# Decode block with grouped-query attention: value product 512 columns wide on two groups of 64 output partitions, and 21 instead of 14 rows of w_down summed 512 columns wide

## The chip, the cores and the metric

The kernel runs on one NeuronCore of one Trainium2 chip. The metric is the device time of one launch in microseconds (us), lower is better. The kernel before takes 437.93 us, the median of 3 runs (437.82 to 437.97).

## What is computed

One decode step of a transformer block for 8 batch rows of width 1024. A modulation product turns `c` into six shift, scale and gate rows; then come attention with a key/value cache, and a gated feed-forward part:

```python
mod = silu(c) @ w_mod                        # 1024 x 6144: sa, ca, ga, sb, cb, gb
h = layernorm(x) * (1 + ca) + sa
q = h @ wq                                   # 32 heads of 128
scores = einsum('bhqd,bhkd->bhqk', q, k) * 128 ** -0.5   # 4 kv heads, 8192 positions, 8 query heads each
o = einsum('bhqk,bhkd->bhqd', softmax(scores), v)
x = x + ga * (o @ wo)
h = layernorm(x) * (1 + cb) + sb
gate = h @ W_gate; up = h @ W_up             # 1024 x 3584
x = x + gb * ((gate * (gate > 0) * up) @ W_down)         # 3584 x 1024
```

All inputs are bf16. The key and value caches hold 67 MB each, the weights 51.4 MB together, so 185.6 MB are read once.

## The kernel before

**Loading.** SyncE's queue issues every large load, in one fixed order (L347-382, issued at L745), into a ring of five SBUF slots A to E of 32 KB per partition: both halves of wq, both of w_mod, then keys of pair 0, and then for each pair n the keys of n+1 and the values of n; wo's first half stands behind the values of pair 0. After the values of pair 15 come wo's second half, the first halves of W_gate and W_up, the second halves, and w_down in five blocks of 14, 7, 4, 2 and 1 rows (a "row" here is one of 28 chunks of 128 contraction rows, `WD`, L380). A load waits until TensorE's last use of what lay in its place before: the keys of pair n+2 until the keys of pair n have been transposed, the values of n+2 until the value product of n is done, wo's second half until the keys of pair 14 are done, the first half of W_gate until the keys of pair 15 are. The queue is served in order, so what stands behind a waiting load waits too.

**Attention.** A pair is one batch row and two of the four key/value heads: 16 pairs, each with 4.19 MB of keys and as much of values. The loop (L646-682) has 18 turns; 16 of them run as a hardware loop of 8 rounds with two turns each, and two more follow without keys. Turn n works on three pairs at once. It transposes the keys of pair n on TensorE, 128 transposes in 16 slots of 8 (`slot_keys`), which VectorE and ScalarE copy out alternately; after every second slot it forms scores (`slot_scores`: 4 products of 512 columns, each writing 32 output partitions of one PSUM bank). It runs the softmax of pair n-1 in slots 2 to 8 (`soft_max` to `turn_p`), and the value product of pair n-1 from slot 9 on (`pv`, eight calls, the last two in slot 15). And it finishes pair n-2: `pv_evac` in slot 0 (two VectorE operations from PSUM bank W into `od`), `o_sum` in slot 2 (TensorE, which needs `od`), `o_evac` in slot 3. The order on every engine is the order in which the code records the operations. The calls in odd slots 9, 11, 13 and 15 stand right behind four score products.

**Value product.** The probabilities are transposed into `pt`, 16 blocks t of 128 positions' columns. For each t four products run, one per group of 32 output partitions, each with 32 columns of `pt` as weights and 256 columns of values (L616-619). Of each result only one 128-column half belongs to the right positions; `pv_evac` masks with `diag` and sums the two halves (L621-623).

**Feed-forward tail.** Gate and up are multiplied with h as they land (L698-703), the product of relu(gate) and up is transposed into `hmT`. w_down's first 14 rows are summed 512 columns wide in four groups of 32 output partitions (bank Y, L722-726); that sum is copied to `yR` by VectorE, and two TensorE products with `fold` bring it into bank W (L727-729). The other 14 rows, in blocks of 7, 4, 2 and 1, are added in W as four products of 256 columns each (L730-734). Two VectorE operations and four small DMAs write the output (L735-739).

Of the kernel before, what the change touches and what calls it, by code (L numbers as in the profile page):

```python
# [234 lines left out]
def bass_adaLN_cond__gqa_block_cached__glu_gated_reglu__decode_kernel(  # L235
# [33 lines left out]
    with ExitStack() as es:  # L269
        E = es.enter_context  # L270

        def sb(name, shape, dtype):
            return E(nc.sbuf_tensor(name, shape, dtype))
# [24 lines left out]
        nb = sb("nb", [128, 1], f32)  # L298
        P = sb("P", [128, 1088], bf16)
        pt = sb("pt", [128, 2048], bf16)  # L300
        ov = sb("ov", [128, 256], f32)
        od = sb("od", [128, 132], f32)
        rl = sb("rl", [128, 1], f32)
        tm = sb("tm", [128, 128], f32)
        sel = sb("sel", [128, 128], f32)
        selo = sb("selo", [128, 128], f32)
        sel16 = sb("sel16", [128, 16], f32)
        diag = sb("diag", [128, 2, 128], bf16)
        blk = sb("blk", [128, 8, 16], f32)
        pick = sb("pick", [128, 2, B], f32)  # L310
        fold = sb("fold", [128, 2, 128], f32)
# [115 lines left out]
        def dve(name, *args, reads=(), writes=(), **kw):  # L427
            return g.op("dve", lambda e: getattr(e, name)(*args, **kw), reads, writes)  # L428
# [19 lines left out]
        def spread(view, n, tile, key, axes=AX.X):  # L448
            dve("tensor_reduce", sel16[:, 0:n], view, axes, ALU.add, reads=["identf"], writes=["sel16"])
            dve("tensor_copy", tile[:].rearrange("p (a z) -> p a z", a=n) if len(tile.shape) == 2 else tile[:],  # L450
                sel16[:, 0:n, None].to_broadcast([128, n, tile.shape[-1] if len(tile.shape) == 3 else tile.shape[-1] // n]),
                reads=["sel16"], writes=[key])

        spread(identf[:].rearrange("p (g y h) -> p g h y", g=2, y=8), 16, sel, "sel")
        spread(identf[:].rearrange("p (q g i h) -> p g h q i", q=4, g=2, i=2), 16, selo, "selo", AX.XY)
        spread(identf[:].rearrange("p (q i r) -> p i q r", q=8, i=2), 2, diag, "diag", AX.XY)
        spread(identf[:].rearrange("p (y k) -> p k y", k=8), 8, blk, "blk")
        dve("tensor_reduce", part[:], identf[:].rearrange("p (q x) -> p q x", q=4), AX.X, ALU.add, reads=["identf"], writes=["part"])
        dve("tensor_reduce", rest[:], identf[:].rearrange("p (q x) -> p x q", q=4), AX.X, ALU.add, reads=["identf"], writes=["rest"])
# [153 lines left out]
        def pv(n, u):  # L613
            v = place[("v", n)].rearrange("p (h j q e) d -> p h q e j d", h=2, j=4, q=2)
            for t in (2 * u, 2 * u + 1):
                for q in range(4):  # L616
                    at = 32 * (4 * t + q)
                    mm(W[32 * q:32 * (q + 1), 0:256], pt[:, at:at + 32], v[:, t // 8, q // 2, t % 8, 2 * (q % 2):2 * (q % 2) + 2, :],
                       t == 0, t == 15, [("pt", t // 8, 0), ("pt", t // 8, 1)], [pW], ("v", n))

        def pv_evac(n):  # L621
            dve("tensor_tensor", out=ov[:, 0:256], in0=W[:, 0:256], in1=diag[:].rearrange("p i d -> p (i d)"), op=ALU.mult, reads=[pW, "diag"], writes=["ov"])
            dve("tensor_reduce", od[:, 0:128], ov[:, 0:256].rearrange("p (i d) -> p d i", i=2), AX.X, ALU.add, reads=["ov"], writes=["od"])

        def o_sum(n):
            mm(W[:, 0:128], selo[:], od[:, 0:128], True, True, ["selo", "od"], [pW])
# [92 lines left out]
        def hm(r):  # L719
            return hmT[:, r // 4, r % 4, :]  # L720

        for t in range(14):  # L722
            w = place[("wd", 0)][:, t, :]
            for h in range(2):
                at = 64 * (t % 2) + 32 * h
                mm(Y[at:at + B, :], hm(t), w[:, 512 * h:512 * (h + 1)], t < 2, t >= 12, [("hmT", 0)], [pY], ("wd", 0))
        dve("tensor_copy", yR[:], Y, reads=[pY], writes=["yR"])  # L727
        for i in range(2):
            mm(W[:, 0:256], fold[:, i], yR[:, 256 * i:256 * (i + 1)], i == 0, False, ["yR", "fold"], [pW])
        for u, (lo, hi, _) in enumerate(WD[1:], 1):  # L730
            for r in range(lo, hi):
                for q in range(4):
                    mm(W[32 * q:32 * q + B, 0:256], hm(r), place[("wd", u)][:, r - lo, 256 * q:256 * (q + 1)], False, r == KF - 1,
                       [("hmT", r // 16)], [pW], ("wd", u))
# [47 lines left out]
```

## Time and profile before

| | |
|---|---|
| median of 3 runs | 437.93 us |
| span of the profiled execution, first to last instruction | 436.1 us |
| TensorE matmul busy | 305.4 us (70%) |
| VectorE busy, ScalarE busy | 180.2 us (41%), 208.6 us (48%) |
| HBM read, mean rate over the span | 185.63 MB, 426 GB/s |
| share of the 16 DMA engines taken by the load queue | 98.8% |

The profiled execution is told by its span; what lies around it is not on the page, and the median of the runs is 1.8 us above the span. Three views carry the rest. The timeline lists instructions in order of time, merged when they are alike (`x8` is eight in a row), with the idle time before them and what ended it. The view of windows gives busy time per engine, granted TensorE clock and DMA rate in stretches of the span. The chain lists what ended last, step by step. In all of them L420 is the helper that records every product, L424 the one for transposes, L428 VectorE's and L431 ScalarE's, so instructions are told apart by their tiles: `ring,pt` is the value product, `KT,Z` the scores, `identb,ring` the key transposes, `ring,hmT` w_down.

### The profile page before, as it was taken

The numbers are of one execution on the slowest core, as the hardware profiler recorded it, in microseconds if no ns is written. First come the engines' busy times: TensorE is split into PE (matmuls) and PEld (weight loads), VectorE is DVE, ScalarE is ACT, GpSimd is POOL, SyncE is SP. The second block draws the span as 40 slices with busy tenths as digits, with TensorE's granted clock in tenths as the row PEclk, the third lists the DMA queues.
The fourth block names the chain that finished last, engine by engine and source line by source line (L and its number), as shares of the span: only waits on it lengthen the run. The fifth ranks groups of instructions, "written<-read, shape, count | busy, mean of one in ns | idle before, by whom it ended". The sixth has DMA issues, their size and how long they took to land.

```text
span 436.1 us, 10694 instructions
## 1 busy us (share of the span) xinstructions
PE 305.4 (70%) x4560; PEld 199.2 (46%) x4560; DVE 180.2 (41%) x385; ACT 208.6 (48%) x246; POOL 12.6 (3%) x52
## 2 busy tenths in 40 slices
PE   0104257989878888787888888777888878754463
PEld 0101025656555555554555555555555555431321
DVE  3600036456363644536264553536364453331111
ACT  2200005576756747675664757576575747400000
POOL 6000000000000000000000000000000000000000
PEclk9999599999999999999999999999999999885778
DMA  8999999999999999999999999999999999999996
GB/s 346 440 437 437 428 431 432 431 434 428 436 433 433 433 433 433 433 436 433 433 433 433 433 433 433 433 433 433 439 436 433 436 433 433 424 428 429 442 416 253
DMA packets 6874, 185.80 MB, mean 426 GB/s; under 512 B 800, under 2 KB 832, under 8 KB 1104
## 3 DMA queue, kind: packets, MB, share of 16 engines
q1 hardware_dynamic: 6800, 185.61, 98.8%
q8 instruction: 8, 0.13, 0.1%
q10 hardware_dynamic: 64, 0.04, 0.0%
q14 instruction: 2, 0.02, 0.0%
HBM read 185.63 MB, written 0.02 MB: 426 GB/s over the span
## 4 chain that ended last, share of the span: by engine, by line
DMA 58%; PE 20%; issue 8%; DVE 7%; ACT 5%; SPq 1%; DVEq 0%; ACTq 0%
DMA ring<-in_A_k_cache_dram 34%; DMA ring<-in_w_mod_dram 11%; PE PS L424 11%; PE PS L420 10%; DMA ring<-in_B_W_up_dram 6%; DMA ring<-in_B_W_down_dram 6%; ACT P L431 3%; DVE KT L428 2%; ACT KT L431 2%; DVE tm L428 1%; DVE ov L428 1%; DVE nm L428 1%; SPq L745 1%; DVE nb L428 0%; DVE rl L428 0%
## 5 line engine op out<-in xcount | busy, mean ns | idle before, releaser
L431 ACT ACTIVATE KT<-PS 128x1024 bf16<-128x1024 bf16 (+1 forms) x130 | 132.1, 1017 | 165.8 <-PE PS L424 137.6
L424 PE MATMUL PS<-identb,ring 128*128 128x128 bf16 x2048 | 152.9, 220 | 21.8 <-DMA ring<-in_A_k_cache_dram 20.1
L428 DVE COPY KT<-PS 128x1024 bf16<-128x1024 bf16 (+1 forms) x129 | 88.9, 689 | 164.3 <-PE PS L424 128.9
L424 PEld LDWEIGHTS PS<-identb,ring 128*128 128x128 bf16 x2048 | 117.0, 98 | 61.0 <-issue 36.9
L420 PE MATMUL PS<-KT,Z 128*32 128x512 bf16 x516 | 51.9, 389 | 0.1
L420 PE MATMUL PS<-ring,pt 128*32 128x256 bf16 x1088 | 49.9, 274 | 0.3 <-DVE pt L428 0.3
L431 ACT ACTIVATE P<-PS,nb 64x1024 bf16<-64x1024 f32 x34 | 37.7, 1108 | 6.2 <-DVE nb L428 4.2
L424 PE MATMUL PS<-identb,P 128*128 128x128 bf16 x272 | 21.6, 225 | 20.2 <-ACT P L431 14.5
L420 PEld LDWEIGHTS PS<-ring,pt 128*32 128x32 bf16 x1088 | 24.4, 95 | 12.7 <-issue 0.5
L420 PE MATMUL PS<-ring,siluT 128*24 128x512 bf16 x96 | 9.1, 555 | 27.4 <-DMA ring<-in_w_mod_dram 27.4
L424 PEld LDWEIGHTS PS<-identb,P 128*128 128x128 bf16 x272 | 16.0, 100 | 26.5 <-DVE KT L428 17.2
L431 ACT ACTIVATE pt<-PS 64x512 bf16<-64x512 bf16 x34 | 20.1, 591 | 13.5 <-PE PS L424 13.3
L428 DVE COPY pt<-PS 64x512 bf16<-64x512 bf16 x34 | 14.4, 422 | 17.4 <-PE PS L424 16.9
L428 DVE TENSOR_REDUCE mp<-PS 128x1 f32<-128x1024 f32 x17 | 20.6, 1214 | 0.0
L420 PE MATMUL PS<-ring,h2T 128*8 128x512 bf16 x112 | 12.0, 545 | 11.9 <-DMA ring<-in_B_W_up_dram 10.1
L420 PEld LDWEIGHTS PS<-KT,Z 128*32 128x32 bf16 x516 | 13.3, 92 | 13.8 <-ACT KT L431 0.5
L420 PEld LDWEIGHTS PS<-ring,siluT 128*24 128x24 bf16 x96 | 3.0, 124 | 33.2 <-DMA ring<-in_w_mod_dram 28.1
L431 ACT ACT_TABLE_LOAD x11 | 14.1, 1283 | 8.5 <-DMA KT<-in_A_x_dram 8.3
L424 PE MATMUL PS<-identb,KT 128*128 128x128 bf16 (+1 forms) x20 | 1.9, 218 | 18.0 <-DVE KT L428 18.0
L635 POOL CAST ot<-og 128x16 bf16<-128x16 f32 x16 | 4.1, 253 | 290.5 <-DVE og L428 290.5
L420 PEld LDWEIGHTS PS<-ring,h2T 128*8 128x8 bf16 x112 | 3.4, 104 | 19.8 <-DMA ring<-in_B_W_up_dram 11.5
L420 PE MATMUL PS<-od,selo 128*128 128x128 f32 x36 | 8.8, 326 | 5.1 <-DVE od L428 5.1
(99 smaller groups left out, 157.5 us busy)
## 6 DMA issues: line engine op xcount, KB each, us to landing
ring<-in_A_k_cache_dram SPq DMA_DIRECT2D x16, 4096.0 KB, 21.6
ring<-in_A_v_cache_dram SPq DMA_DIRECT2D x16, 4096.0 KB, 30.5
ring<-in_w_mod_dram SPq DMA_DIRECT2D x2, 6144.0 KB, 42.5
ring<-in_A_wq_dram SPq DMA_DIRECT2D x2, 4096.0 KB, 16.9
ring<-in_A_wo_dram SPq DMA_DIRECT2D x2, 4096.0 KB, 29.4
ring<-in_B_W_gate_dram SPq DMA_DIRECT2D x2, 3584.0 KB, 25.0
ring<-in_B_W_up_dram SPq DMA_DIRECT2D x2, 3584.0 KB, 31.1
ring<-in_B_W_down_dram SPq DMA_DIRECT2D x1, 3584.0 KB, 37.6
```

Source lines behind the costliest of these rows:

```text
L420: return pe(lambda e: e.matmul(out_, lhsT, rhs, start=start, stop=stop, skip_group_check=True), reads, writes, block, deps)
L424: return pe(lambda e: e.matmul(out_, in_, ident, start=True, stop=True, is_transpose=True), reads, writes, block)
L428: return g.op("dve", lambda e: getattr(e, name)(*args, **kw), reads, writes)
L431: return g.op("act", lambda e: e.activation(*args, **kw), reads, writes)
L635: pool(lambda e: e.tensor_copy(dst, og[:, n % 2]), reads=[("og", n % 2)], writes=[("ot", n // B)])
L745: o.fn = (lambda e, key=key, src=src, o=o: e.dma_start(place[key], src).then_inc(o.sem, 16))
```

## The change

For each block t the value product is two products instead of four: 64 columns of `pt` as weights, 64 output partitions, 512 columns of values. The bank W then holds four 128-column parts per partition of which one belongs to it. So `ov` and `diag` are twice as wide, `pv_evac` masks 512 columns and sums four parts, and the mask is built by two reductions and two multiplications at the start instead of one reduction and one copy. In the tail, w_down's rows 0 to 20 (its first two blocks) are summed 512 columns wide in bank Y, and the copy to `yR` and the two `fold` products follow row 20 instead of row 13; rows 21 to 27 stay as they were. TensorE's program, loop counted once, is 2,015 instructions long, by 220 shorter than before.

```diff
-        ov = sb("ov", [128, 256], f32)
+        ov = sb("ov", [128, 512], f32)
-        diag = sb("diag", [128, 2, 128], bf16)
+        diag = sb("diag", [128, 2, 2, 128], bf16)
+        pair = sb("pair", [128, 2, 2], f32)
...
-        spread(identf[:].rearrange("p (q i r) -> p i q r", q=8, i=2), 2, diag, "diag", AX.XY)
+        dve("tensor_reduce", pair[:, 0], identf[:].rearrange("p (q a r) -> p a q r", q=2, a=2), AX.XY, ALU.add, reads=["identf"], writes=["pair0"])
+        dve("tensor_reduce", pair[:, 1], identf[:].rearrange("p (q i r) -> p i q r", q=8, i=2), AX.XY, ALU.add, reads=["identf"], writes=["pair1"])
+        for a in range(2):
+            dve("tensor_scalar", out=diag[:, a], in0=pair[:, 1, :, None].to_broadcast([128, 2, 128]), scalar1=pair[:, 0, a:a + 1], scalar2=None,
+                op0=ALU.mult, reads=["pair0", "pair1"], writes=["diag"])
...
-                for q in range(4):
-                    at = 32 * (4 * t + q)
-                    mm(W[32 * q:32 * (q + 1), 0:256], pt[:, at:at + 32], v[:, t // 8, q // 2, t % 8, 2 * (q % 2):2 * (q % 2) + 2, :],
+                for q in range(2):
+                    at = 64 * (2 * t + q)
+                    mm(W[64 * q:64 * (q + 1), :], pt[:, at:at + 64], v[:, t // 8, q, t % 8],
                        t == 0, t == 15, [("pt", t // 8, 0), ("pt", t // 8, 1)], [pW], ("v", n))
...
-            dve("tensor_tensor", out=ov[:, 0:256], in0=W[:, 0:256], in1=diag[:].rearrange("p i d -> p (i d)"), op=ALU.mult, reads=[pW, "diag"], writes=["ov"])
-            dve("tensor_reduce", od[:, 0:128], ov[:, 0:256].rearrange("p (i d) -> p d i", i=2), AX.X, ALU.add, reads=["ov"], writes=["od"])
+            dve("tensor_tensor", out=ov[:], in0=W[:], in1=diag[:].rearrange("p a i d -> p (a i d)"), op=ALU.mult, reads=[pW, "diag"], writes=["ov"])
+            dve("tensor_reduce", od[:, 0:128], ov[:].rearrange("p (i d) -> p d i", i=4), AX.X, ALU.add, reads=["ov"], writes=["od"])
...
-        for t in range(14):
-            w = place[("wd", 0)][:, t, :]
+        for t in range(21):
+            u = t // 14
+            w = place[("wd", u)][:, t % 14, :]
             for h in range(2):
                 at = 64 * (t % 2) + 32 * h
-                mm(Y[at:at + B, :], hm(t), w[:, 512 * h:512 * (h + 1)], t < 2, t >= 12, [("hmT", 0)], [pY], ("wd", 0))
+                mm(Y[at:at + B, :], hm(t), w[:, 512 * h:512 * (h + 1)], t < 2, t >= 19, [("hmT", t // 16)], [pY], ("wd", u))
...
-        for u, (lo, hi, _) in enumerate(WD[1:], 1):
+        for u, (lo, hi, _) in enumerate(WD[2:], 2):
```

## The prediction, made before the result was known

> **What bounds the kernel now.** I read the page first (queues, 40 slices), then the waits of SyncE's queue and its timeline, then TensorE's and VectorE's timeline of one turn of the loop.
>
> ```profile
> q1 hardware_dynamic: 6800, 185.61, 98.8%
> HBM read 185.63 MB, written 0.02 MB: 426 GB/s over the span
> 0.00:2.00 2.00, 0.00 (x0) 0.00 (x0) 0.00 (x0) 0.00 (x0) 1.47 (x12) 1.00 0.67 188
> 254.00:292.00 38.00, 30.95 (x488) 21.03 (x481) 18.49 (x38) 24.76 (x29) 0.67 (x4) 1.00 1.01 438
> ```
>
> The load queue fills 98.8% of the span. So the time changes only if the last load lands at another time, or if the work behind it does. The queue starves only if TensorE frees a slot too late. SyncE's timeline tells how late it is now:
>
> ```profile
> 83.17 0.33 SPq L745 DMA_DIRECT2D ring<-in_A_k_cache_dram  x1
> 100.90 0.33 SPq L745 DMA_DIRECT2D ring<-in_A_k_cache_dram  x1
> 118.64 0.33 SPq L745 DMA_DIRECT2D ring<-in_A_k_cache_dram  x1
> 332.15 19.62 SPq L745 DMA_DIRECT2D ring<-in_A_v_cache_dram  x2
> 370.10 0.33 SPq L745 DMA_DIRECT2D ring<-in_B_W_gate_dram  x1
> ```
>
> The first three rows are the moments at which the keys of pairs 0, 1 and 2 are used up: 17.73 and 17.74 us apart. There TensorE runs behind the loads and at its own pace, so one turn of its own takes 17.73 us. Later one turn takes 19.36 us ((370.10 - 118.64) / 13 = 19.34 to the keys of pair 15), which is 8.39 MB at 433 GB/s (19.4 us). TensorE has 1.6 us per turn to spare:
>
> ```profile
> L424 PE MATMUL PS<-identb,ring 128*128 128x128 bf16 x1800 | 134.4, 220 | 20.1 <-DMA ring<-in_A_k_cache_dram 20.1
> ```
>
> That row covers the 14 turns from 100 to 370 us: 20.1 / 14 = 1.4 us of waiting for keys per turn. The whole question is whether a turn grows by more than that.
>
> **The value product.** One stretch of a turn at TensorE's own pace:
>
> ```profile
> 91.02 0.40 PE L420 MATMUL PS<-KT,Z 128*32 128x512 bf16 x4
> 91.35 0.62 PE L424 MATMUL PS<-identb,ring 128*128 128x128 bf16 x8
> 94.84 0.40 PE L420 MATMUL PS<-KT,Z 128*32 128x512 bf16 x4
> 95.07 0.39 PE L420 MATMUL PS<-ring,pt 128*32 128x256 bf16 x8
> 95.39 0.62 PE L424 MATMUL PS<-identb,ring 128*128 128x128 bf16 x8
> 95.94 0.40 PE L420 MATMUL PS<-ring,pt 128*32 128x256 bf16 x8
> 96.28 0.62 PE L424 MATMUL PS<-identb,ring 128*128 128x128 bf16 x8
> 96.83 0.40 PE L420 MATMUL PS<-KT,Z 128*32 128x512 bf16 x4
> 101.03 0.61 PE L420 MATMUL PS<-ring,pt 128*32 128x256 bf16 x16
> 101.57 1.07 PE L424 MATMUL PS<-identb,ring 128*128 128x128 bf16 x16
> ```
>
> No row from 94.84 to 101.57 has a wait: here TensorE is the bound, and what it gets more to do lengthens the turn. Four products on four groups of 32 partitions run side by side. Two such fours of 256 columns take 95.39 - 95.07 = 0.32 us, four of them 101.57 - 101.03 = 0.54, so one four costs 0.11 and the last of a run 0.21. A four of 512 columns costs 0.22 ahead of a product of the same form (94.84 to 95.07) and 0.33 ahead of a transpose (91.02 to 91.35). So the time goes by columns per group, and as before each group's columns are streamed beside the others'. Now a block t has 512 columns in each of two groups, where it had 256 in each of four: with both groups side by side a block costs 0.22 instead of 0.11. Fewer, wider products fill half the groups and take twice the time. A call behind a transpose or ahead of one: 0.22 + 0.33 = 0.55 instead of 0.33, +0.22; six such per turn, +1.32. The double call in slot 15: 3 x 0.22 + 0.33 = 0.99 instead of 0.54, +0.45. Together **+1.77 us per turn**.
>
> **The change of form between scores and values.** In three places of these rows TensorE goes from one array form (128 columns of weights, or 32) to the other, and each costs about 0.10 us more: 0.33 - 0.22 and 0.21 - 0.11 into a transpose; and eight transposes take 0.55 up to the next product (95.39 to 95.94), where sixteen take 1.07 with the last one's 0.22, so 0.45 for eight. Scores into values now keep the form (32 and 32) and pay nothing. After the change they go from 32 to 64, four times a turn. No row shows 32 to 64: the lower bound is 0, the upper 0.10 each. I take 0.10, since every change of form that the rows show pays it: **+0.40 us per turn**. The Trainium skill, TensorEngine Tiling (Array Packing), Key Properties, says that changing the tiling mode, and not just the tile, drains TensorE; the rows agree for 128 against 32, and by that rule this step is charged, without it the sum below comes to 442.1.
>
> **The evacuation.** It is on TensorE's path:
>
> ```profile
> 102.84 0.41 DVE L428 TENSOR_TENSOR ov<-PS,diag 128x256 f32<-128x256 f32 x1
> 103.29 0.42 DVE L428 TENSOR_REDUCE od<-ov 128x128 f32<-128x256 f32 x1
> 103.76 0.30 PEld L420 LDWEIGHTS PS<-od,selo 128*128 128x128 f32 x2 [0.42 <-DVE od L428]
> 421.19 1.28 DVE L428 TENSOR_TENSOR KT<-PS,KT 128x512 bf16<-128x512 f32 x2 [11.53 <-PE PS L420]
> L428 DVE TENSOR_REDUCE mp<-PS 128x1 f32<-128x1024 f32 x14 | 17.0, 1214 | 0.0
> ```
>
> `o_sum` waits 0.42 us for `od`, and behind it on TensorE stand the transposes of slot 3 and the softmax's steps. A multiplication of 512 columns takes 1.28 / 2 = 0.64 us, 0.23 over 0.41. A reduction of 1024 takes 1.21, of 256 0.42, so 512 takes 0.42 + 0.79 / 3 = 0.68, 0.26 over. **+0.5 us per turn**, all of it a longer wait.
>
> So a turn takes 17.73 + 1.77 + 0.40 + 0.5 = 20.40 us, over the 19.36 that the loads need.
>
> **What that does to the end.** TensorE starts turn 0 at 66.03. The values of pair 15 are issued when the product of pair 13 ends, which is the end of turn 14; before, that is 332.15 + 19.62 - 0.33 = 351.44, with 1.6 us to spare before turn 15's keys.
>
> ```profile
> 66.03 1.06 PE L424 MATMUL PS<-identb,ring 128*128 128x128 bf16 x16 [1.74 <-DVE qT L428]
> 394.30 1.02 PE L420 MATMUL PS<-ring,h2T 128*8 128x512 bf16 x7 [1.87 <-DVE h2T L428]
> ```
>
> After the change turn 14 ends at 66.0 + 15 x 20.40 = 372.0. Behind it the queue has the values of pair 15, wo's second half, gate and up, and w_down: 2 x 4.19 + 4 x 3.67 + 7.34 = 30.4 MB, 70.2 us at 433 GB/s. From issue to first data I take 1 us, between 0.4 (first issue at 0.74, and 188 GB/s over the first 2 us put the first byte near 1.1) and 1.9 (issue of the output at 434.24 to the end at 436.1). The last load lands at 372.0 + 1.0 + 70.2 = 443.2. Before, it was there at 432.99 (row below), so **+10.2 us**. The break-even turn is (433.0 - 71.2 - 66.0) / 15 = 19.72 us; each 0.1 us per turn beyond it costs 1.5 us.
>
> All other loads behind that are issued in time: the first gate load needs the keys of pair 15 (turn 15's end at 392.4 less about 1.2, so 391.2), and wo's half lands at 392.4. TensorE's first h2T product comes 21.7 us later than at 394.30 through the loop and some 2.7 through the last value product and two evacuations, 418.7; up's last half lands at 426.3, so there is time for the first halves, and for w_down's second block, which the gate's first half frees near 425 (56 products of 0.107), long before the queue needs it at 434.8.
>
> **The tail and the rest.**
>
> ```profile
> 424.46 1.68 PE L420 MATMUL PS<-ring,hmT 128*8 128x512 bf16 x28 [1.51 <-DMA ring<-in_B_W_down_dram]
> 426.20 0.69 DVE L428 COPY yR<-PS 128x512 f32<-128x512 f32 x1 [3.00 <-PE PS L420]
> 426.94 1.13 PE L420 MATMUL PS<-yR,fold 128*128 128x256 f32 x4 [0.80 <-DVE yR L428]
> 431.12 0.61 PE L420 MATMUL PS<-ring,hmT 128*8 128x256 bf16 x16 [1.47 <-DMA ring<-in_B_W_down_dram]
> 432.99 0.28 PE L420 MATMUL PS<-ring,hmT 128*8 128x256 bf16 x4 [0.24 <-DMA ring<-in_B_W_down_dram]
> 415.92 5.24 PE L420 MATMUL PS<-ring,h2T 128*8 128x512 bf16 x49 [6.38 <-DMA ring<-in_B_W_up_dram]
> 409.80:420.00 10.20, 4.08 (x37) 1.31 (x40) 0.00 (x0) 0.00 (x0) 0.00 (x0) 0.50 1.02 439
> 423.40:426.80 3.40, 1.68 (x28) 0.59 (x28) 0.60 (x1) 0.00 (x0) 0.00 (x0) 1.00 0.97 416
> 2.13 49.52 DMA ring<-in_w_mod_dram
> q8 instruction: 8, 0.13, 0.1%
> ```
>
> Now the copy and the fold stand behind w_down's second block, which lands 1.84 MB (4.2 us) ahead of the last, at 439.0. Its 14 products take 14 x 0.06 = 0.84, the copy with its waits 0.8, the fold 1.13: done at 441.8. The block of four rows, there at 441.4, is waited for by 0.4 us, its products end at 442.4, and the next rows land at 442.6. So at full clock the tail is hidden with 0.2 us to spare: +0. But between the first and the second block TensorE now idles some 2.6 us where the fold stood. The wait of 1.51 left the clock whole (1.00 from 423.4 on), the one of 6.38 ahead of 415.92 came with 0.50 granted, and products at 5.24 / 49 = 0.107 instead of 0.06. At half clock the steps take 1.6 + 0.8 + 2.3 and the 28 products behind them about 2.4, an end at 446.1 instead of 443.5: up to +2.6. I take 0, since 2.6 us is nearer to 1.51.
>
> The longer build of `diag` (two operations more, at most about 0.7 us from the 0.42 and 0.41 above) lies on VectorE while w_mod lands until 51.65; uncovered it would cost that 0.7. The removed products and weight loads gain nothing by number: their time is in the rows above.
>
> **Sum.** The span goes from 436.1 to 446.3 us. The median of the runs is 1.8 us above the profiled span, so **448.1 us**, 2.3% slower.
>
> **Rivals.** *The change of form is free*: a turn takes 20.00 us, the last load lands at 437.2, +4.2, **442.1 us**. For it speaks that scores and values both use parts of the array, so weights might be set early; against it, every change seen costs 0.10. *The turn stays under 19.72 us*, and nothing is lost: **437.9 us**. This is the other side: the value product's wider streams would have to cost 0.7 us less than worked out, in waits that TensorE has anyway. Such waits stand in slots 0 to 8 (0.42 for `od`), not in the stretch with the value product, which speaks against it. *Two groups of 64 partitions do not run side by side*: 32 products of 0.22 instead of 16 steps, +3.5 us per turn on 20.00, 23.5 us, 66.0 + 352.5 + 71.2 = 489.7, +56.7, **about 495 us**. No row has 64-wide groups; against it, four 32-wide ones overlap well. *The program's length*: the 8 packets of queue 8 load instructions, 0.13 MB or 0.3 us of the queue; if they vanish, and no turn grows, 0.3 us are won, **437.6 us**. The Trainium skill, Runtime: NRT & Kernel Launch, Instruction fetch mechanics, gives TensorE room for 2,048 instructions, refilled in blocks of 256; by that rule 2,015 would fit, and 8 packets agree with some 2,235 before.
>
> **Chances.** The sum as worked out 0.60, with a range of its own of 446.5 to 451 (the turn good to 0.1 us, the tail up to 2.6). Form change free or half priced 0.26 (442.1 to 446.5). Hidden 0.07. Groups one after the other 0.05. Faster 0.02, all of it the program's length. The range 442 to 451.5 leaves out the last three. What a measurement can tell from no change is 0.2%, 0.9 us; that gives faster 0.02, same 0.07, slower 0.91.
>
> **What would show it.** The keys of successive pairs used up about 20.4 us apart all through the loop (19.9 to 20.1 for the second case); no wait of the key transposes for keys; value products of 512 columns with the transposes about 0.55 us behind their start, and about 0.3 instead of 0.23 between scores and values; a wait of about 0.9 us for `od`; DMA shares below 1.00 from about the tenth turn on; in the tail only waits for w_down, unless the clock shows 0.50. I am wrong if the keys are still waited for in turns 3 to 15.

## The result: 459.78 us, and the profile after

The changed kernel takes 459.78 us, the median of 5 runs (457.17 to 460.84), beside 437.91 us for the kernel before on the same chip: a ratio of 1.049, with a 95% interval of 1.047 to 1.050. It is slower, as forecast, but by 21.9 us where 10.2 were forecast, and outside the range of 442 to 451.5. The profiled execution took 458.93 us and has a span of 457.2 us, 21.1 more than before.

First the page of the changed kernel (queues, and groups of instructions with busy time, mean ns, idle time before them and what ended it). In the changed kernel the helpers stand a line later: L421 records products, L425 transposes, L429 VectorE's operations, and the loads are issued at L751.

```profile
q1 hardware_dynamic: 6800, 185.61, 96.2%
q8 instruction: 8, 0.13, 0.1%
HBM read 185.63 MB, written 0.02 MB: 406 GB/s over the span
L425 PE MATMUL PS<-identb,ring 128*128 128x128 bf16 x2048 | 152.9, 220 | 1.7 <-DVE qT L429 1.7
L421 PE MATMUL PS<-od,selo 128*128 128x128 f32 x36 | 8.8, 326 | 21.0 <-DVE od L429 21.0
L429 DVE TENSOR_REDUCE od<-ov 128x128 f32<-128x512 f32 x18 | 18.4, 1020 | 0.6
L429 DVE TENSOR_TENSOR ov<-PS,diag 128x512 f32<-128x512 f32 x18 | 12.3, 682 | 5.6 <-PE PS L421 5.6
```

The load queue moves the same bytes, but no longer fills the span. The key transposes, which waited 20.1 us for keys before, wait for none. TensorE waits 21.0 us for `od` instead, because the reduction into it takes 1.02 us and the multiplication ahead of it 0.68. The 8 packets of instruction loading are still there.

SyncE's timeline of the changed kernel (start, length, and how often it is issued):

```profile
87.24 0.33 SPq L751 DMA_DIRECT2D ring<-in_A_k_cache_dram  x1
108.04 0.33 SPq L751 DMA_DIRECT2D ring<-in_A_k_cache_dram  x1
...
357.69 0.33 SPq L751 DMA_DIRECT2D ring<-in_A_k_cache_dram  x1
359.01 21.14 SPq L751 DMA_DIRECT2D ring<-in_A_v_cache_dram  x2
```

From 87.24 to 357.69 there are 13 turns: 20.80 us each, all alike. So TensorE sets the pace from the first turn to the last, at 20.80 us a turn instead of the 20.40 forecast. In most turns from the third on the share of the DMA engines is below 1.00 (0.96 from 130 to 150 us), where the prediction said from about the tenth. A window of the next turn (busy time per engine, then granted clock, DMA share and GB/s):

```profile
150.00:171.00 21.00, 18.18 (x220) 11.03 (x220) 10.34 (x19) 13.25 (x16) 0.34 (x2) 1.00 0.96 401
```

The values of pair 15 are issued at 359.01 + 21.14 - 0.33 = 379.82 us (forecast 372.0).

TensorE's timeline of the same kernel, the start, three stretches of a turn, and the tail:

```profile
59.76 4.96 PE L421 MATMUL PS<-ring,hT 128*16 128x512 bf16 x64 [1.85 <-DVE hT L429]
67.65 1.06 PE L425 MATMUL PS<-identb,ring 128*128 128x128 bf16 x16 [1.74 <-DVE qT L429]
...
100.32 0.40 PE L421 MATMUL PS<-KT,Z 128*32 128x512 bf16 x4
100.65 0.62 PE L421 MATMUL PS<-ring,pt 128*64 128x512 bf16 x4
101.20 0.62 PE L425 MATMUL PS<-identb,ring 128*128 128x128 bf16 x8
...
108.27 1.05 PE L421 MATMUL PS<-ring,pt 128*64 128x512 bf16 x8
109.25 1.07 PE L425 MATMUL PS<-identb,ring 128*128 128x128 bf16 x16
112.31 0.49 PE L421 MATMUL PS<-od,selo 128*128 128x128 f32 x2 [1.11 <-DVE od L429]
...
447.70 1.68 PE L421 MATMUL PS<-ring,hmT 128*8 128x512 bf16 x28
449.83 1.03 PE L421 MATMUL PS<-ring,hmT 128*8 128x512 bf16 x14 [0.45 <-DMA ring<-in_B_W_down_dram]
451.65 1.13 PE L421 MATMUL PS<-yR,fold 128*128 128x256 f32 x4 [0.79 <-DVE yR L429]
454.09 0.28 PE L421 MATMUL PS<-ring,hmT 128*8 128x256 bf16 x4 [0.22 <-DMA ring<-in_B_W_down_dram]
```

A call of the value product takes 101.20 - 100.65 = 0.55 us, the double one 0.98, and scores into values 100.65 - 100.32 = 0.33, where it was 0.23. All three are as forecast. The wait for `od` is 1.11 us (forecast 0.9). Of the tail's loads only w_down is waited for. The last products start 21.1 us later than before (454.09 against 432.99), which is the whole growth of the span: the work behind the last load has not changed.

### The profile page after: what moved, and what is told of

Its sections match the earlier page's. It is cut to its first block, busy times and chain, and to the rows that moved or that the text cites. A ratio compares the mean times of both kernels' runs of the same rounds, so it can differ in the third digit from the quotient of the medians.

```text
span 457.2 us, 9580 instructions
## 1 busy us (share of the span) xinstructions
PE 345.2 (76%) x4002; PEld 202.4 (44%) x4002; DVE 196.1 (43%) x387; ACT 208.5 (46%) x246; POOL 12.6 (3%) x52
## 4 chain that ended last, share of the span: by engine, by line
PE 46%; issue 15%; DMA 15%; DVE 15%; ACT 9%; SPq 1%; DVEq 0%; ACTq 0%; POOL 0%
PE PS L421 28%; PE PS L425 18%; DMA ring<-in_w_mod_dram 11%; ACT P L432 5%; DMA ring<-in_B_W_down_dram 4%; ACT KT L432 4%; DVE KT L429 4%; DVE ov L429 3%; DVE tm L429 2%; DVE nm L429 1%; DVE mp L429 1%; DVE rl L429 1%; DVE od L429 1%; DVE nb L429 1%; SPq L751 1%
## 5 line engine op out<-in xcount | busy, mean ns | idle before, releaser
L429 DVE COPY KT<-PS 128x1024 bf16<-128x1024 bf16 (+1 forms) x129 | 89.0, 690 | 177.9 <-PE PS L425 142.5
L425 PE MATMUL PS<-identb,ring 128*128 128x128 bf16 x2048 | 152.9, 220 | 1.7 <-DVE qT L429 1.7
L425 PEld LDWEIGHTS PS<-identb,ring 128*128 128x128 bf16 x2048 | 117.0, 98 | 62.3 <-issue 55.5
L421 PE MATMUL PS<-ring,pt 128*64 128x512 bf16 x544 | 80.3, 389 | 0.4 <-DVE pt L429 0.4
L421 PE MATMUL PS<-KT,Z 128*32 128x512 bf16 x516 | 51.5, 389 | 0.0
L425 PE MATMUL PS<-identb,P 128*128 128x128 bf16 x272 | 21.5, 224 | 20.1 <-ACT P L432 14.4
L421 PEld LDWEIGHTS PS<-ring,pt 128*64 128x64 bf16 x544 | 21.5, 108 | 24.4 <-issue 15.1
L421 PE MATMUL PS<-ring,siluT 128*24 128x512 bf16 x96 | 10.0, 599 | 26.5 <-DMA ring<-in_w_mod_dram 26.5
L425 PEld LDWEIGHTS PS<-identb,P 128*128 128x128 bf16 x272 | 15.9, 100 | 26.4 <-DVE KT L429 17.1
L432 ACT ACTIVATE pt<-PS 64x512 bf16<-64x512 bf16 x34 | 20.1, 591 | 14.1 <-PE PS L425 13.9
L421 PE MATMUL PS<-od,selo 128*128 128x128 f32 x36 | 8.8, 326 | 21.0 <-DVE od L429 21.0
L429 DVE COPY pt<-PS 64x512 bf16<-64x512 bf16 x34 | 14.4, 422 | 18.1 <-PE PS L425 17.6
L429 DVE TENSOR_REDUCE mp<-PS 128x1 f32<-128x1024 f32 x17 | 20.7, 1215 | 0.0
L421 PEld LDWEIGHTS PS<-KT,Z 128*32 128x32 bf16 x516 | 13.2, 92 | 13.7 <-issue 0.4
L429 DVE TENSOR_REDUCE od<-ov 128x128 f32<-128x512 f32 x18 | 18.4, 1020 | 0.6
L421 PEld LDWEIGHTS PS<-ring,siluT 128*24 128x24 bf16 x96 | 3.1, 129 | 33.1 <-DMA ring<-in_w_mod_dram 27.5
L421 PEld LDWEIGHTS PS<-od,selo 128*128 128x128 f32 x36 | 5.4, 188 | 24.6 <-DVE od L429 24.6
L425 PE MATMUL PS<-identb,KT 128*128 128x128 bf16 (+1 forms) x20 | 1.9, 217 | 18.3 <-DVE KT L429 18.3
L429 DVE TENSOR_TENSOR ov<-PS,diag 128x512 f32<-128x512 f32 x18 | 12.3, 682 | 5.6 <-PE PS L421 5.6
```

The costliest lines, as they stand in the source:

```text
L421: return pe(lambda e: e.matmul(out_, lhsT, rhs, start=start, stop=stop, skip_group_check=True), reads, writes, block, deps)
L425: return pe(lambda e: e.matmul(out_, in_, ident, start=True, stop=True, is_transpose=True), reads, writes, block)
L432: return g.op("act", lambda e: e.activation(*args, **kw), reads, writes)
```

## The experiments

Each short diff is against the kernel named ahead of it. "Turn" is the distance between two moments at which the keys of successive pairs are used up, read from SyncE's timeline. The kernel before took 437.89 to 437.92 us in the median beside all of these.

**Part by part: w_down alone.** The kernel before with nothing but the tail's part of the change:

```diff
-        for t in range(14):
+        for t in range(21):
...
-        for u, (lo, hi, _) in enumerate(WD[1:], 1):
+        for u, (lo, hi, _) in enumerate(WD[2:], 2):
```

> The kernel before with only the w_down part of the change (rows 0 to 20 summed 512 columns wide). Theory A (all of the loss is TensorE's longer turn in the attention loop): the last load lands where it did, the copy and the fold end before the rows behind them arrive, 437.9 us within 0.9. Rival B (part of the loss is the tail: copy and fold behind the second w_down block, or a lower clock there): 438.5 to 440.5 us, with the last w_down products later than 0.3 us behind the last landing.

438.79 us (437.87 to 439.69), ratio 1.002, interval 1.0011 to 1.0029. TensorE's timeline of the tail, and one window of this kernel (busy times per engine, then granted clock, DMA share and GB/s):

```profile
424.47 1.68 PE L420 MATMUL PS<-ring,hmT 128*8 128x512 bf16 x28 [1.86 <-DMA ring<-in_B_W_down_dram]
428.72 1.03 PE L420 MATMUL PS<-ring,hmT 128*8 128x512 bf16 x14 [2.56 <-DMA ring<-in_B_W_down_dram]
430.54 2.08 PE L420 MATMUL PS<-yR,fold 128*128 128x256 f32 x4 [0.79 <-DVE yR L428]
432.54 1.66 PE L420 MATMUL PS<-ring,hmT 128*8 128x256 bf16 x28
```

```profile
429.64:433.00 3.36, 2.57 (x18) 1.50 (x20) 0.69 (x1) 0.00 (x0) 0.00 (x0) 0.50 0.66 267
```

TensorE idles 2.56 us between w_down's first two blocks, where the fold stood before. Behind that the clock is at 0.50: the fold takes 2.08 us instead of 1.13, and the last 28 products run as one row without a wait, so they and not the load set the end. That is rival B's sign; the time alone lies in the ranges of both theories. The part costs 0.9 us by itself. The runs show that price; that it is the half clock is read from this one profile. Half the clock in the tail is not peculiar to this kernel: with the form alone (below), whose tail is the old one, the fold took 2.08 us too (from 427.54), and its last products still waited 0.18 us for their load (at 433.34). I had taken 0 out of "up to +2.6", and that step was wrong for this kernel.

**Part by part: the value product alone.** The changed kernel with w_down's old tail:

```diff
-        for t in range(21):
+        for t in range(14):
...
-        for u, (lo, hi, _) in enumerate(WD[2:], 2):
+        for u, (lo, hi, _) in enumerate(WD[1:], 1):
```

> The changed kernel with w_down as before (14 rows 512 wide), so only the value product and its evacuation are changed. Theory A: all of the loss, turns of 20.8 us, 457 to 461 us. Rival B: less than 457 us by what the tail costs.

460.1 us (459.98 to 461.34), ratio 1.0516, interval 1.050 to 1.053; a turn of 20.80 us. The two intervals touch at 1.050, and the full change is not the slower of the two: all of the measurable loss comes from the value product and its evacuation. In the full change w_down's part costs nothing more that can be measured: in its profiled execution TensorE came late to w_down's first block (no wait at 447.70), and waited only 0.45 us for the second.

**The sum of the four parts by additions.** The changed kernel, with two additions in the place of the reduction:

```diff
-            dve("tensor_reduce", od[:, 0:128], ov[:].rearrange("p (i d) -> p d i", i=4), AX.X, ALU.add, ...)
+            dve("tensor_tensor", out=ov[:, 0:256], in0=ov[:, 0:256], in1=ov[:, 256:512], op=ALU.add, ...)
+            dve("tensor_tensor", out=od[:, 0:128], in0=ov[:, 0:128], in1=ov[:, 128:256], op=ALU.add, ...)
```

> The changed kernel, but the four masked parts are summed by two additions (256 and 128 columns wide) instead of one reduction of 512, which took 1.02 us where 0.68 was forecast. Theory A: additions of about 0.41 and 0.3 us, so a turn is shorter by about 0.3 us (20.5), and the end comes 15 times that earlier, 4.5 to 5 us: 454 to 456 us. Rival C (the end is set by what the load queue loses at each restart, not by the turn): within 1 us of the changed kernel, 458 to 461 us.

453.22 us (452.9 to 455.96), ratio 1.037, interval 1.034 to 1.040. VectorE's timeline of this kernel:

```profile
87.54 0.68 DVE L429 TENSOR_TENSOR ov<-PS,diag 128x512 f32<-128x512 f32 x1
88.26 0.43 DVE L429 TENSOR_TENSOR ov<-ov 128x256 f32<-128x256 f32 x1
88.72 0.29 DVE L429 TENSOR_TENSOR od<-ov 128x128 f32<-128x128 f32 x1
```

The turn is 20.54 us, 0.26 shorter, and 15 x 0.26 = 3.9 us. Of the other 2.1 us of the 6.0 between the two profiled spans (457.2 and 451.2), 1.9 are the start: turn 0 begins at 65.73 here and at 67.65 in the changed kernel. The 454 to 456 us expected had left the start out. So the reduction does stand on TensorE's path with all that it takes, and part of the 21.9 us is not the turn's but the start's.

**Four groups of 32, 512 columns wide.** The changed kernel with the old array form for the value product:

```diff
-                for q in range(2):
-                    at = 64 * (2 * t + q)
-                    mm(W[64 * q:64 * (q + 1), :], pt[:, at:at + 64], v[:, t // 8, q, t % 8],
+                for q in range(4):
+                    at = 32 * (4 * t + q)
+                    mm(W[32 * q:32 * (q + 1), :], pt[:, at:at + 32], v[:, t // 8, q // 2, t % 8],
```

> The changed kernel, but the value product on four groups of 32 output partitions, each 512 columns wide, as the scores are: the same columns per group, four products per block instead of two, the same evacuation, no change of form between scores and values. Theory A: four groups side by side take the time of two, 0.22 us a block, and 4 x 0.11 us per turn of form change go: a turn of 20.37 us, 6.6 us earlier, 452 to 455 us. Rival D (it is the number of columns written in all that costs, so twice as many products cost twice): a turn of 20.37 + 3.5 = 23.9 us, over 500 us. Rival E (the 0.11 us is not the change of form but the value product's own start): 458 to 461 us.

452.15 us (449.84 to 454.14), ratio 1.032, interval 1.028 to 1.036. TensorE's timeline of this kernel, the same place in a turn:

```profile
100.77 0.40 PE L421 MATMUL PS<-KT,Z 128*32 128x512 bf16 x4
101.00 0.60 PE L421 MATMUL PS<-ring,pt 128*32 128x512 bf16 x8
101.53 0.62 PE L425 MATMUL PS<-identb,ring 128*128 128x128 bf16 x8
```

Eight products on four groups take 0.53 us, and four on two groups took 0.55: the time goes by the columns of one group, whether it holds 32 or 64 partitions. Scores into values is back at 0.23, and the turn at 20.31 us, 0.50 shorter. So the change of form costs 0.50 us a turn, and twice as many instructions cost nothing.

**The three terms, each alone on the kernel before.** First the columns alone, with the old evacuation:

```diff
-                    mm(W[32 * q:32 * (q + 1), 0:256], pt[:, at:at + 32], v[:, t // 8, q // 2, t % 8, 2 * (q % 2):2 * (q % 2) + 2, :],
+                    mm(W[32 * q:32 * (q + 1), :], pt[:, at:at + 32], v[:, t // 8, q // 2, t % 8],
```

> The kernel before, with each value product 512 columns wide instead of 256, still on four groups of 32 output partitions; the evacuation stays 256 wide, so for half of the heads it masks columns that hold other positions' products, and those heads' values are left out of the sum. Only the columns term remains. Theory A (the turn's terms add, and nothing shows before a turn passes about 19.5 us): a turn of 17.73 + 1.77 = 19.50 us at TensorE's own pace, right at the break-even, so 437.9 to 440 us, and hardly any waiting for keys. Rival F (any longer turn delays the loads in proportion): 15 x 1.77, about 464 us.

Then the evacuation alone, behind the old product, with `ov` 512 wide and `diag` held twice:

```diff
-            dve("tensor_tensor", out=ov[:, 0:256], in0=W[:, 0:256], in1=diag[:].rearrange("p i d -> p (i d)"), ...)
-            dve("tensor_reduce", od[:, 0:128], ov[:, 0:256].rearrange("p (i d) -> p d i", i=2), AX.X, ALU.add, ...)
+            dve("tensor_tensor", out=ov[:], in0=W[:], in1=diag[:].rearrange("p a i d -> p (a i d)"), ...)
+            dve("tensor_reduce", od[:, 0:128], ov[:].rearrange("p (i d) -> p d i", i=4), AX.X, ALU.add, ...)
```

> The kernel before, with the evacuation 512 wide (mask of 512 columns, reduction of four parts, two of them always zero), the value product unchanged. Only the evacuation's term remains. Theory A: VectorE's two operations take 0.68 and 1.02 us, the turn at TensorE's own pace is 17.73 + 0.87 = 18.60 us, below the 19.36 us of the loads: 437.9 us within 0.5, and 0.76 us of waiting for keys per turn instead of 1.4 to 1.6. Rival F: 15 x 0.87, about 451 us.

And the form alone, 64 columns of weights but 256 columns of values:

```diff
-                for q in range(4):
-                    at = 32 * (4 * t + q)
-                    mm(W[32 * q:32 * (q + 1), 0:256], pt[:, at:at + 32], v[:, t // 8, q // 2, t % 8, 2 * (q % 2):2 * (q % 2) + 2, :],
+                for q in range(2):
+                    at = 64 * (2 * t + q)
+                    mm(W[64 * q:64 * (q + 1), 0:256], pt[:, at:at + 64], v[:, t // 8, q, t % 8, 0:2, :],
```

> The kernel before, with the value product on two groups of 64 output partitions but only 256 columns wide, so half of the positions' values are left out; the evacuation as before. Only the change of form remains. Theory A: two calls' blocks take what they took (0.11 us each), and only the step from scores to values grows, from 0.23 to 0.33 us, four times a turn: 18.1 to 18.2 us per turn between the first key loads, 437.9 us in all. Rival E (it is the number of weight columns per product that costs, not the change): every call grows, also those behind a transpose, by some 0.1 us, a turn of 18.6 us.

Columns alone: 437.92 us (437.8 to 440.79), ratio 1.0018, interval 1.0002 to 1.0034. Evacuation alone: 438.0 us (437.85 to 439.69), ratio 1.000, interval 0.9991 to 1.0009. Form alone: 438.26 us, one run. The profiled execution of the evacuation alone is the slowest of its ten (439.69; the others 437.85 to 438.19). Key transposes of the kernel with columns alone, over its turns from 100 to 370 us, and then a stretch of TensorE's timeline of the kernel with the form alone:

```profile
L424 PE MATMUL PS<-identb,ring 128*128 128x128 bf16 x1779 | 132.8, 220 | 0.0
```

```profile
98.15 0.40 PE L420 MATMUL PS<-KT,Z 128*32 128x512 bf16 x4
98.48 0.41 PE L420 MATMUL PS<-ring,pt 128*64 128x256 bf16 x4
98.82 0.62 PE L424 MATMUL PS<-identb,ring 128*128 128x128 bf16 x8
```

Each term gets its price from the turn at TensorE's own pace, which was (118.64 - 83.17) / 2 = 17.735 us before:

| | turn, us | more than before | forecast |
|---|---|---|---|
| columns alone | 19.435 | +1.70 | +1.77 |
| form alone | 18.235 | +0.50 | +0.40 |
| evacuation alone | 18.595 | +0.86 | +0.5 |
| sum | | +3.06 | +2.67 |
| the change | 20.80 | +3.07 | +2.67 |

The terms add up to 0.01 us. Alone, the form and the evacuation are hidden: their turns lie well under the loads' 19.36 us. Columns alone come out right at the edge: keys are never waited for, the median is unmoved, and the runs fall into two groups, eight at 437.8 to 438.0 and four at 439.7 to 440.8 (of the 23 runs of the kernel before beside them, one is that late, at 439.43).

**What a reduction costs.** The kernel before with VectorE operations on old data put in while w_mod lands; strided parts lie 128 elements apart as in the changed kernel:

```diff
...
+        probe("sa", strided(128, 2))
+        probe("sb", strided(128, 3))
+        probe("sc", strided(128, 4))
+        probe("sd", strided(128, 8))
+        probe("se", strided(64, 4))
+        probe("sf", strided(64, 8))
+        probe("ca", wf[:, 0:256].rearrange("p (d i) -> p d i", i=2))
+        probe("cb", wf[:, 0:512].rearrange("p (d i) -> p d i", i=4))
+        probe("pa", wf[:, 0:544].rearrange("p (i d) -> p d i", i=4)[:, 0:128, :])
+        for n in (128, 256, 512):
+            dve("tensor_tensor", out=yR[:, 0:n], in0=wf[:, 0:n], in1=wf[:, 512:512 + n], op=ALU.add, ...)
```

> The kernel before, with reductions and additions of several shapes on VectorE while w_mod lands, which nothing reads: reductions of 2, 3, 4 and 8 parts of 128 columns, of 4 and 8 parts of 64, of 2 and 4 neighbouring elements, of 4 parts 136 columns apart, and additions of 128, 256 and 512 columns. Of the changed kernel 4 parts of 128 took 1.02 us, 2 took 0.42. Theory G (a part of a reduction costs as much per element whatever the shape, and two parts are a special, cheap case): 3 parts 0.7 to 0.8 us, 4 parts 1.0, 8 parts 1.8 to 2.2. Rival H (the distance of 128 columns between four parts collides): the 136 apart, or 4 neighbouring elements, take about 0.7 us. Time: 437.9 us, since nothing waits for it.

Groups of VectorE's instructions of this kernel, shapes kept apart; `tm` takes the strided sums, `gbR` those of neighbouring elements, `x1R` the one with parts 136 apart, `yR` the additions:

```profile
L428 DVE TENSOR_REDUCE tm<-wide 128x128 f32<-128x1024 f32 x1 | 1.9, 1872 | 0.0
L428 DVE TENSOR_REDUCE tm<-wide 128x128 f32<-128x512 f32 x1 | 1.0, 1018 | 0.0
L428 DVE TENSOR_REDUCE x1R<-wide 128x128 f32<-128x512 f32 x1 | 1.0, 1016 | 0.0
L428 DVE TENSOR_REDUCE gbR<-wide 128x128 f32<-128x512 f32 x1 | 0.7, 686 | 0.0
...
L428 DVE TENSOR_REDUCE tm<-wide 128x128 f32<-128x384 f32 x1 | 0.6, 593 | 0.0
...
L428 DVE TENSOR_REDUCE gbR<-wide 128x128 f32<-128x256 f32 x1 | 0.4, 419 | 0.0
L428 DVE TENSOR_REDUCE tm<-wide 128x128 f32<-128x256 f32 x1 | 0.4, 361 | 0.0
```

Two strided parts of 128 take 0.36 us (0.42 in the loop of the kernel before), three 0.59, four 1.02, eight 1.87. From four to eight a strided element costs (1872 - 1018) / 512 = 1.67 ns; neighbouring ones cost (686 - 419) / 256 = 1.04 ns, and 512 of them take 0.69 us, which is what the prediction had interpolated. So the strided order is the reason: the same 512 elements cost 1.02 us in one order and 0.69 in the other. With 64 sums instead of 128, four parts took 0.58 us and eight 1.01, so from four parts on the time goes by the elements read. The expectation that a strided part always costs the same was wrong for three (0.59 us, 0.7 to 0.8 expected). Parts 136 apart cost the same as 128 apart, so the distance of 128 by itself is not the reason.

**Both repairs.** The changed kernel with four groups of 32 and with the two additions:

> Two repairs at once: four groups of 32 partitions, 512 columns wide (no change of form, a turn of 20.31 us measured), and the parts summed by two additions (0.26 us less per turn measured). Theory A (the terms add): a turn of 20.31 - 0.26 = 20.05 us; against the four groups alone 15 x 0.26 = 3.9 us less, 446 to 450 us. If the terms overlap, 449 to 453 us.

451.17 us (446.4 to 452.21), ratio 1.026, interval 1.021 to 1.031. The turn is 20.05 us, just 20.31 - 0.26, so the two repairs add up. The median is above the 446 to 450 us that go with terms that add, although the turn shows that they do. In the profiled execution (span 449.9, against 457.2 of the changed kernel) 15 x 0.76 = 11.4 us are won in the loop. 1.06 are given back at the start (turn 0 at 68.71), 2.1 because w_down's second block comes 72.2 us behind the values of pair 15 (issued at 369.48) instead of 70.0, and 0.9 in the tail:

```profile
441.63 1.03 PE L421 MATMUL PS<-ring,hmT 128*8 128x512 bf16 x14 [2.56 <-DMA ring<-in_B_W_down_dram]
443.45 2.07 PE L421 MATMUL PS<-yR,fold 128*128 128x256 f32 x4 [0.79 <-DVE yR L429]
```

This is the fold at half clock again, as with w_down alone: in this execution w_down's part had a price again.

**TensorE kept busy.** Two kernels put products in that nobody reads: 50 of them ahead of the loop of the changed kernel, and 10 between w_down's first two blocks in the kernel with w_down alone. The cut shows 40 of the first kernel's 50 (the other 10 stand behind the modulation product), and then the second kernel's 10.

```diff
...
+                for _ in range(40):
+                    mm(bank(6), identb[:], P[:, 0:512], True, True, ["identb", ("P", 0)], [pB[6]])
...
+            if t == 14:
+                for _ in range(10):
+                    mm(bank(6), identb[:], P[:, 0:512], True, True, ["identb"], [pB[6]])
```

> The changed kernel, with 50 idle products before the loop, 40 while the second half of w_mod lands and 10 while VectorE works behind it, whose results nothing reads. They only keep TensorE busy. Theory I (the runs of the changed kernel differ by 3.7 us because TensorE's granted clock at the q projection is sometimes 0.50, which moves the start of the loop from 66.0 to 67.6 and with it everything behind): the loop starts at 66.0 +- 0.4 in every run, 457 us median, runs within 1.5 us of each other. Rival J (the spread comes from the tail or from the loads): 458 to 461 us as before, and a spread of 3 us.

459.14 us (457.18 to 460.41), ratio 1.047, interval 1.043 to 1.050. This did not do what it should. The q projection runs at full clock (3.63 us), but the inserted products hold back the modulation product ahead of it (52.94 instead of 51.52), turn 0 still begins at 67.40, and the clock is at 0.50 from 53.6 to 57.0 and from 67.3 to 70.7. It moved the half clock and did not remove it, and the runs spread nearly as wide as before (3.2 us, 3.7 without). So it says nothing on whether the start's clock makes the runs differ.

> The w_down part alone, which took 438.79 us, with ten idle products between w_down's first and second block, whose results nothing reads. Theory K (the 0.9 us is the clock of 0.50 behind the 2.56 us of idling where the fold stood): the fold takes 1.13 us instead of 2.08, and the time is 437.9 us within 0.3. Rival L (it is the fold's later place): 438.5 to 439.0 us as without the idle products.

438.3 us (437.76 to 441.22), ratio 1.0006, interval 0.999 to 1.002. TensorE's timeline of the tail of this kernel (of the 10 inserted products the trace has 9):

```profile
424.53 2.94 PE L420 MATMUL PS<-ring,hmT 128*8 128x512 bf16 x28 [1.08 <-DMA ring<-in_B_W_down_dram]
427.81 2.31 PE L420 MATMUL PS<-P,identb 128*128 128x512 bf16 x9 [0.33 <-issue]
430.05 1.03 PE L420 MATMUL PS<-ring,hmT 128*8 128x512 bf16 x14
431.87 1.13 PE L420 MATMUL PS<-yR,fold 128*128 128x256 f32 x4 [0.79 <-DVE yR L428]
```

The fold is back at 1.13 us. But the half clock did not go: here it fell on the 28 products of w_down's first block, which took 2.94 us instead of 1.68. The inserted products, begun late, then held w_down's 14 back, from 428.72 to 430.05. The median lies between the times that went with the two theories (437.9 and 438.5 to 439.0), and the interval of the ratio holds no loss as well as the whole of the 0.9 us. So whether the idle stretch and its clock make w_down's price is not settled.

## Why the prediction was right in direction and wrong in size

The mechanism was the one forecast; the sizes of three terms were not. The turn rose past what the loads need, the queue starved, the values of pair 15 were issued late, and the last load with the span by the same amount. "The turn stays under 19.72 us" and "two groups do not run side by side" fell with the turn of 20.80; a free change of form fell with the kernel that has the form alone (+0.50). The longer build of `diag` cost nothing at the start: the kernel with additions has it and began turn 0 at 65.73. The program's length won nothing that shows, and the 8 packets of instruction loads did not vanish. The Trainium skill, Runtime: NRT & Kernel Launch, Instruction fetch mechanics, gives TensorE room for 2,048 instructions. The page of the profile shows 8 packets with 2,015 as with 2,235, and not whose instructions they carry.

The profiled span was forecast at 446.3 us and is 457.2. The 10.9 us between them are in these steps, the first the largest:

- **The evacuation, "+0.5 us per turn".** It is +0.86. The multiplication was near (0.68 for 0.64). The reduction was interpolated between one of two strided parts (256 elements, 0.42) and one of 1024 neighbouring elements (1.21), which gave 0.68, and it takes 1.02. This is the step that failed: a price for strided parts was drawn partly from a row that reads neighbours. It makes 15 x 0.36 = 5.4 us by itself. With the form at +0.50 for +0.40 and the columns at +1.70 for +1.77, the turn comes out 0.40 too short, and 15 turns make **6.1 us** of it.
- **"TensorE starts turn 0 at 66.03."** It started at 67.65, **1.6 us** later. The q projection took 4.96 us instead of 3.63, with the clock at 0.50, as the first row of the next fence shows, and it began 0.3 later. In the kernel with additions it took 3.63 again, and the loop began at 65.73. So the start varies between executions of kernels with the same code ahead of the loop, and the prediction had taken one execution's start as a constant.
- **The term "from issue to first data I take 1 us" and "70.2 us at 433 GB/s".** From 379.82 to the last landing at about 454.1 pass 74.3 us, not 71.2: **3.1 us**. The queue's flat rate was the mistake:

Windows of the changed kernel (granted clock, DMA share and GB/s are the last three columns; the last row is the end of the one above it):

```profile
59.10:62.50 3.40, 2.74 (x28) 1.08 (x32) 0.45 (x2) 0.00 (x0) 0.00 (x0) 0.50 1.08 463
378.00:380.00 2.00, 2.00 (x25) 1.05 (x24) 0.10 (x1) 1.02 (x1) 0.00 (x0) 1.00 0.00 0
380.00:386.00 6.00, 4.66 (x65) 3.25 (x61) 5.52 (x10) 2.11 (x3) 0.25 (x1) 1.00 0.91 350
424.00:454.10 30.10, 23.29 (x235) 12.03 (x235) 6.62 (x20) 1.29 (x3) 0.00 (x0) 0.77 0.94 398
448.00:454.10 6.10, 4.48 (x73) 1.79 (x65) 0.71 (x2) 0.00 (x0) 0.00 (x0) 1.00 0.74 301
```

and of the kernel before a window, and its q projection:

```profile
403.00:433.00 30.00, 16.41 (x202) 8.47 (x193) 3.82 (x8) 1.08 (x2) 0.00 (x0) 0.83 0.95 406
59.47 3.63 PE L420 MATMUL PS<-ring,hT 128*16 128x512 bf16 x64 [1.85 <-DVE hT L428]
```

The queue is empty from 378 to 380, and its first 6 us move 350 GB/s; against 433 that is 6 x 83 / 433 = 1.2 us, and 0.2 us had passed since the issue: 1.4 for the 1 us forecast. The last 30 us move 398 GB/s, which loses 30.1 x 35 / 433 = 2.4 us; 6.1 x 132 / 433 = 1.9 of them are lost in the last 6.1 us, at 301 GB/s with the DMA engines busy for 0.74 of the time. So it is mostly the end of the stream that is slow. That row could be had from the trace of before: its last 30 us ran at 406, and its last 6 at 330. Together 2.8 of the 3.1 us.

With the median, the forecast of 448.1 us was 11.7 too low; the other 0.8 are that the profiled execution (458.93 us) lies below the median.

The two last points also move the break-even: with 74.3 us behind the issue it is (433.0 - 74.3 - 66.0) / 15 = 19.51 us, not 19.72, and with a start at 67.65 it is 19.40. Columns alone, at 19.44 with a start at 65.84 and no loss in the median, agree with the first.

**The tail, "+0".** For the full change this held in the profiled execution, by luck: the reason given did not hold. The prediction took 2.6 us of idling as near enough to 1.51 to leave the clock whole; with w_down alone the same idle stretch came with half the clock, and the part cost 0.9 us. In the full change's profile the stretch did not arise, since TensorE came late. In that of the kernel with 50 inserted products, whose loop and tail are the same, it did (2.36 us), with the fold at full clock (1.13).

**The form.** The Trainium skill, TensorEngine Tiling (Array Packing), Key Properties, says that a change of the tiling mode drains TensorE. The traces fit that for 32 against 64 columns too: 0.33 instead of 0.23 us between scores and values, and 0.50 us a turn for the four places, 0.12 each.

What stays open: the runs of the changed kernel differ by 3.7 us, where those of the kernel before beside them agree to 0.2. In the profiled executions turn 0 begins between 65.73 (additions), 68.59 (four groups) and 68.71 (both repairs), the late ones with a q projection of 5.32 us. A kernel that no longer waits for loads hands such a late start on to its end. Even a kernel bound by loads seems to: in the late execution with the evacuation alone the q projection took 6.51 us, turn 0 began at 69.05, and from 86 to 96 us the queue moved 393 GB/s where it moved 441 before. That this makes all of the spread, or the four late runs with columns alone, was not shown.

None of the kernels tried is faster than the kernel before.

## What to carry to other kernels

When a kernel is bound by its loads but an engine has only a little slack per turn, cost each edit against that slack, and take the sum: three edits that were hidden or at the edge alone (437.9, 438.0 and 438.3 us) made 21.9 us together. Products that are wider on fewer groups save instructions and not time, since TensorE's time went by the columns of one group. A price for an operation is taken from a row with the same access pattern, or measured by a probe put under a wait; and a rate for the queue from the stretch in which it will be used, its end above all, not from its middle.

## What the runs showed of the hardware

- A VectorE reduction of strided parts costs by parts in an uneven way: 128 sums of 2, 3, 4 and 8 parts took 0.36, 0.59, 1.02 and 1.87 us, while the four-part sum took 0.69 over neighbouring elements, and 0.43 + 0.29 = 0.72 by two additions.
- Eight products of 32 output partitions and four of 64, all of 512 columns, took 0.53 and 0.55 us: two groups run side by side as four do.
- An idle stretch of 2.56 us ahead of w_down's second block was followed by half the granted clock in two profiled executions (the fold at 2.08 and 2.07 us), and one of 2.55 in the kernel with four groups was not (the fold at 1.13). So the length of the stretch alone does not decide it. In these profiles the granted clock changes only at moments that lie whole multiples of 3.41 us apart (in the changed kernel at 55.7, 59.1 and 62.5, for one). Of the 3.41 us ahead of such a moment TensorE's products were busy for 0.92 us with w_down alone (426.23 to 429.64) and for 1.04 with both repairs (440.05 to 443.46), and the clock fell; for 1.62 with the 50 inserted products (446.14 to 449.56) and for 1.68 in the kernel before (423.47 to 426.88), and it stayed whole. Near 1.5 both came: 1.47 with four groups (439.42 to 442.84) left it whole, 1.49 with the 10 inserted products (421.39 to 424.80) did not. So where a stretch lies between these moments counts beside its length.
